# Attention and a feed-forward layer in one kernel: weights' sign by a leaky ReLU in whole words, chunks made when due, TensorE transposes for the second group

## The chip, the core and the metric

The kernel runs on one core of a Trainium2 chip. A core has five engines that run side by side and wait for each other through semaphores: PE (TensorE, matmul), DVE (VectorE), ACT (ScalarE), POOL (GpSimd) and SP (SyncE, which here issues every DMA). The metric is device time of one execution in microseconds (us).

## The reference

```python
def _attn_ref(q, k, v):                      # B, H, S, D = 8, 8, 576, 64
    scores = matmul(q, k.T) / sqrt(D)
    rel = pos[:, None] - pos[None, :]
    mask_local = (rel >= 0) & (rel < 32)                 # heads 0 to 3
    mask_strided = (rel >= 0) & (same position mod 32)   # heads 4 to 7
    attn = softmax(where(mask, scores, -1e9))
    return matmul(attn, v)

def reference(q, k, v, w_in, w_out):
    x = attn_out as (4608, 512)
    h = x @ w_in                             # (512, 2048)
    g = h * sigmoid(1.702 * h)
    return g @ w_out                         # (2048, 512)
```

The two weight matrices come as float64 (q, k and v as float32).

## The kernel before

**Feed-forward.** The 4608 tokens are cut into 12 groups of 384, the 2048 hidden units into 16 blocks of 128. One *step* is one block for one group: `ffn1` is 12 matmuls of 384 columns into a bank `h`, `act` makes `g` from it (tanh on ACT, a product on DVE) and splits it into a high part `gh` (ACT) and a low part `gl` (POOL in the first 8 steps, else DVE), and two steps later `ffn2` is 9 matmuls of 512 columns into three banks `o`. There are 192 steps, first 8 blocks of group 0, then the 16 of group 1, then the other 8 of group 0, then group after group.

**Attention.** It is done in 48 *pairs* of blocks of queries, and each group needs four pairs on average. A pair goes through: `scores` (PE, into `s`; mask and row maximum on DVE), `softmax` (eight Exp on ACT with a row sum each; `rinv` on DVE; a product on POOL), `transpose` of `pr` into `pt`, and `values` (PE, into `a`; ACT and DVE split it into the high and low inputs `xh`, `xl` of `ffn1`; a last letter `l` or `s` tells local from strided). Two buffers `pr` take turns. Pairs 0 to 4 (group 0) are done ahead of the steps and use TensorE transposes (`t`, L206) followed by a DVE copy (L210); the later ones use DVE's own 32x32 block transposes (L220). Pairs 5 to 9, which group 1 needs, are transposed at steps 1 to 5; pairs 10 and 11 are transposed from step 25 on.

**Weights.** They come in 32 *chunks* (w_in and w_out alternating, 16 each; 128 rows of 512 doubles). A chunk is loaded as pairs of 32-bit words (`raw`); the high word holds sign, exponent and the top of the mantissa, the low word the rest. `bits_w` makes the low word hold the sign bit at the top and three mantissa bits at the bottom: L299 writes its lower half and L302 its upper half, both on ACT as 16-bit elements at a step of 8 bytes. `join_w` scales the high word as a float into `t` (L312, DVE), which rebases the exponent, and shifts and ORs the two (L316, DVE). `split_w` splits the float32 into a high part (L329, ACT cast to fp32r) and a low part (L330, DVE). A generator does this piece by piece: `fill(n)` advances it by n pieces, three to a chunk.

**Order.** Instructions are recorded in program order and a scheduler with a simulated timeline then orders each engine's queue; from the first step on (`in_order`), PE's matmuls are kept in program order. Each engine executes its queue in order.

Of the kernel before, what the change touches and what calls it, by code (L numbers as in the profile page):

```python
# [9 lines left out]
F32 = mybir.dt.float32  # L10
F32R = mybir.dt.float32r
U32 = mybir.dt.uint32
U8 = mybir.dt.uint8
BF16 = mybir.dt.bfloat16
F16 = mybir.dt.float16
U16 = mybir.dt.uint16
AF = mybir.ActivationFunctionType
ALU = mybir.AluOpType
AX = mybir.AxisListType
# [21 lines left out]
HU = HEADS * U  # L41

AHEAD = 2
LAG = 2
RAWB = 3
NEARLY = 4
PF = (2, 3, 3, 3, 3, 3, 4)
F0F = 6
NH = NF // 2


# [23 lines left out]
def attn_ffn(ctx, tc, qk, vs, w_in, w_out, masks, ident, out):  # L75
    nc = tc.nc
# [20 lines left out]
    pairs, windows, n0 = _pairs()  # L97
    in_order = [False]

    def matmul(*args, **kw):  # L100

        ins = nc.tensor.matmul(*args, **kw)  # L102
        if in_order[0]:
            tc.keep_in_program_order(ins)

# [2 lines left out]
    def load_qk(p):  # L108
        if p < len(pairs) and p not in qks:
            qks[p] = st4([P, 2, 2, U, P], F32, f"qk_{p}")  # L110
            nc.sync.dma_start(out=qks[p], in_=qk[p])
# [10 lines left out]

    prs = [const.tile([P, HU, P], F32, name=f"pr_{i}") for i in range(AHEAD)]
    pts = {
# [15 lines left out]
    def scores(p):  # L140

        nq, nk, mask = geom(p)
        t = qks[p]
        sps = [bank(f"s{j}_{p}") for j in range(2)]
        for g in range(2):
            for u in range(U):
                for j in range(2):
                    rows = slice(j * D, (j + 1) * D)
                    i = g * U + u
                    matmul(  # L150
                        sps[j][:nq, i * nk : (i + 1) * nk],
                        lhsT=t[rows, 0, g, u, :nq],
                        rhs=t[rows, 1, g, u, :nk],
                        start=True,
                        stop=True,
                    )
        scale = 1.0 / np.sqrt(D)
        pr = prs[p % AHEAD]
        n = mask.shape[1]
        for j in range(2):  # L160
            o = pr[:nq, j * 2 * U : (j + 1) * 2 * U, :nk]
            if n == 2:
                o = o.rearrange("p (g u) n -> p g (u n)", g=2)
            nc.vector.scalar_tensor_tensor(
                out=o, in0=sps[j][:nq, : 2 * U * nk].rearrange("p (a n) -> p a n", a=n),
                scalar=scale, in1=mask, op0=ALU.mult, op1=ALU.add,
            )
        nmax = small.tile([P, HU], F32, tag="nmax", name=f"nmax_{p}")
        nc.vector.tensor_reduce(  # L169
            out=nmax[:nq], in_=pr[:nq, :, :nk], axis=AX.X, op=ALU.max, negate=True  # L170
        )
        nmaxs[p] = nmax

    def softmax(p):

        nq, nk, _ = geom(p)
        nmax, pr = nmaxs.pop(p), prs[p % AHEAD]
        ssum = small.tile([P, HU], F32, tag="ssum", name=f"ssum_{p}")
        for i in range(HU):
            nc.scalar.activation(  # L180
                pr[:nq, i, :nk], pr[:nq, i, :nk], AF.Exp,
                bias=nmax[:nq, i : i + 1], scale=1.0,
                accum_out=ssum[:nq, i : i + 1],
            )
            if i % 2 and i < HU - 1:
                yield
        rinv = small.tile([P, HU], F32, tag="rinv", name=f"rinv_{p}")
        nc.vector.tensor_scalar_add(out=rinv[:nq], in0=ssum[:nq], scalar1=1e-9)  # L188
        nc.vector.reciprocal(out=rinv[:nq], in_=rinv[:nq])  # L189
        nc.gpsimd.tensor_tensor(  # L190
            out=pr[:nq, :, :nk],
            in0=pr[:nq, :, :nk],
            in1=rinv[:nq].unsqueeze(2).broadcast_to([nq, HU, nk]),
            op=ALU.mult,
        )

    def transpose(p):
        nq, nk, _ = geom(p)
        kind, pr = pairs[p][0], prs[p % AHEAD]
        pt = pts[kind]  # L200
        if p < n0:
            for j in range(2):
                tps = bank(f"t{j}_{p}")
                heads = slice(j * 2 * U, (j + 1) * 2 * U)
                for i in range(2 * U):
                    nc.tensor.transpose(  # L206
                        tps[:nk, i * nq : (i + 1) * nq], pr[:nq, j * 2 * U + i, :nk],
                        ident_sb[:nq, :nq],
                    )
                nc.vector.tensor_copy(  # L210
                    out=pt[:nk, heads, :nq],
                    in_=tps[:nk, : 2 * U * nq].rearrange("p (h n) -> p h n", h=2 * U),
                )
            return


        for qb in range(-(-nq // BL)):
            for kb in (qb, qb + 1) if kind == "l" else range(max(qb - 1, 0), qb + 1):
                i, o = slice(qb * BL, (qb + 1) * BL), slice(kb * BL, (kb + 1) * BL)
                nc.vector.transpose(out=pt[o, :, i], in_=pr[i, :, o])  # L220
# [53 lines left out]
    raws = {}  # L274

    order = [(f, m) for f in range(NF) for m in range(2)]
# [12 lines left out]

    words = {}  # L290

    def bits_w(i):

        raw = raws[i]
        l16 = raw.bitcast(U16)
        nc.scalar.activation(  # L299
            l16[:, :, 0], raw.bitcast(U8)[:, :, 3], AF.Copy, scale=1 / 32, bias=-15.5 / 32  # L300
        )
        nc.scalar.activation(  # L302
            raw.bitcast(F16)[:, :, 1], raw.bitcast(F32)[:, :, 1], AF.Copy, scale=2.0**-80
        )

    def join_w(i):
        raw = raws.pop(i)
        h, l = raw[:, :, 1], raw[:, :, 0]
        t = words[i] = st2([P, DM], U32, f"t_{i}")


        nc.vector.tensor_scalar_mul(  # L312
            out=t.bitcast(F32), in0=h.bitcast(F32), scalar1=2.0**-112
        )
        yield
        nc.vector.scalar_tensor_tensor(  # L316
            out=t, in0=t, scalar=3, in1=l, op0=ALU.logical_shift_left, op1=ALU.bitwise_or
        )
# [11 lines left out]
        nc.vector.tensor_tensor(out=lo, in0=v, in1=hi.bitcast(F32), op=ALU.subtract)  # L330

    def weights():
        for i in range(RAWB):
            load_w(i)
        bits_w(0)
        for i in range(len(order)):
            if i + 1 < len(order):
                bits_w(i + 1)
            yield from join_w(i)
            yield  # L340
            load_w(i + RAWB)
            split_w(i)
            yield

    wgen = weights()

    def fill(n):
        for _ in range(n):
            next(wgen, None)

    hps = {}

# [14 lines left out]
    def act(j, f):  # L367
# [6 lines left out]
        gh, gl = (  # L374
            ffn.tile([P, G], F32R, tag=f"g{x}", name=f"g{x}_{j}_{f}", bufs=LAG + 1) for x in "hl"
        )
# [51 lines left out]
    def run(gen, n=HU):  # L428
        for _ in range(n):
            next(gen, None)  # L430
# [3 lines left out]
    load_qk(1)  # L434
    ident_sb = const.tile([P, P], F32, name="ident_sb")
    nc.sync.dma_start(out=ident_sb, in_=ident)
    next(wgen)
    for i in range(n0 + 2):
        if i < n0:
            load_qk(i + 1)  # L440
            load_v(i)
            scores(i)
            run(softmax(i))
        if 0 <= i - 2:
            values(i - 2)
        if 0 <= i - 1 < n0:
            transpose(i - 1)
        fill(PF[i])
        if i >= n0 - 2:
            ffn1(0, i - n0 + 2, (0, 1))  # L450
    load_v(n0)
    for p in range(n0, n0 + AHEAD):
        load_qk(p)
        scores(p)
        run(softmax(p))
    load_qk(n0 + AHEAD)

# [6 lines left out]
    due = {}  # L464
    p = n0
# [8 lines left out]

    in_order[0] = True
    late, turn = None, {p: s for s, p in due.items()}
    for s in range(len(steps) + LAG):
        cur = steps[s] if s < len(steps) else None
        old = steps[s - LAG] if s >= LAG else None
        p, q = due.get(s), due.get(s - 1)  # L480
        if cur:
            ffn1(*cur, tuple(range(2 if s < NEARLY else 0, NC)))
            act(*cur)
        if late is not None:
            run(late[0], -(-4 // (late[1] - s)) if late[1] > s else HU)
        if p is not None:
            load_v(p)
            load_qk(p + AHEAD)
            transpose(p)
        if q is not None:  # L490
            values(q)
            load_v(q + 1)
            if q + AHEAD < len(pairs):
                scores(q + AHEAD)
                load_qk(q + AHEAD + 1)
                if late is not None:
                    run(late[0])
                late = softmax(q + AHEAD), turn[q + AHEAD]
                run(late[0], 1)
        fill(F0F)  # L500
        if old:
            for parts in ((0, 1, 2),) if old[1] == NF - 1 else ((0, 1), (2,)):
                for i in range(NT):
                    ffn2(*old, i, parts)
            gs.pop(old)


def _layout(q, k, v, w_in, w_out):
# [73 lines left out]
```

## Time and profile before

| | |
|---|---|
| median of 3 runs | 996.97 us (996.59 to 997.46) |
| the profiled execution | 997.53 us, of which the span is 995.7 us |
| PE busy | 946.0 us, 95% of the span |
| DVE, ACT, POOL busy | 560.2, 453.3, 96.9 us |
| HBM traffic | 54.69 MB read, 9.44 MB written |

The page of the profile shows busy time in 40 slices of 24.9 us each, one digit a slice, in tenths. A group row names line, engine, operation, tiles, shape and count, then the busy time in us and the mean of one instruction in ns, then the idle time of the engine before them and who ended it. The timeline has start, duration, engine, line, tile and count; the chain of waits lists what set the end, in order of time. A table by stages has, for each stretch, its length and each engine's busy time, then the granted TensorE clock (1.00 is full), the DMA engines' busy share and GB/s.

### The profile page before, as it was taken

The numbers are of one execution on the slowest core, as the hardware profiler recorded it, in microseconds if no ns is written. First come the engines' busy times: TensorE is split into PE (matmuls) and PEld (weight loads), VectorE is DVE, ScalarE is ACT, GpSimd is POOL, SyncE is SP. The second block draws the span as 40 slices with busy tenths as digits, with TensorE's granted clock in tenths as the row PEclk, the third lists the DMA queues.
The fourth block names the chain that finished last, engine by engine and source line by source line (L and its number), as shares of the span: only waits on it lengthen the run. The fifth ranks groups of instructions, "written<-read, shape, count | busy, mean of one in ns | idle before, by whom it ended". The sixth has DMA issues, their size and how long they took to land.

```text
span 995.7 us, 14642 instructions
## 1 busy us (share of the span) xinstructions
PE 946.0 (95%) x5608; PEld 834.5 (84%) x5608; DVE 560.2 (56%) x1071; ACT 453.3 (46%) x1334; POOL 96.9 (10%) x64
## 2 busy tenths in 40 slices
PE   4787779999999999999999999999999999999998
PEld 4665568988888888889888888889888888889997
DVE  5789984246665755634555665644555666422322
ACT  6999993224444344332344444332344444322221
POOL 2112220001011011100010110100010110000000
PEclk9997799999999999999999999999999999999999
DMA  8455520011311212210212212110212120000000
GB/s 301 159 191 179 195 83 1 1 62 35 96 41 56 87 41 65 65 32 1 96 32 65 75 54 64 65 32 1 81 47 65 65 64 22 33 1 1 32 1 32
DMA packets 23973, 65.06 MB, mean 65 GB/s; under 512 B 2656, under 2 KB 2912, under 8 KB 23904
## 3 DMA queue, kind: packets, MB, share of 16 engines
q1 hardware_dynamic: 23904, 64.14, 19.5%
q8 instruction: 44, 0.72, 0.3%
q14 instruction: 25, 0.20, 0.1%
HBM read 54.69 MB, written 9.44 MB: 64 GB/s over the span
## 4 chain that ended last, share of the span: by engine, by line
PE 85%; ACT 10%; DVE 3%; issue 1%; DMA 1%; SPq 0%
PE o L102 40%; PE h L102 38%; PE s L102 3%; ACT pr L180 3%; PE a L102 3%; ACT raw L299 3%; ACT raw L302 3%; DVE t L316 1%; DMA raw<-w_in 1%; DVE t L312 1%; ACT o L329 1%; ACT i L329 0%; DVE pt_s L220 0%; DVE pt_l L220 0%; ACT g L370 0%
## 5 line engine op out<-in xcount | busy, mean ns | idle before, releaser
L102 PE MATMUL o<-o,gh 128*128 128x512 f32 x1152 | 312.1, 403 | 8.1 <-ACT gh L377 7.6
L102 PEld LDWEIGHTS o<-o,gh 128*128 128x128 f32 x1152 | 212.9, 190 | 50.0 <-ACT gh L377 8.7
L102 PE MATMUL h<-xhl,i 128*128 128x384 f32 x768 | 234.8, 347 | 1.8 <-DVE g L371 1.4
L102 PE MATMUL h<-xhs,i 128*128 128x384 f32 x768 | 226.8, 336 | 2.2 <-ACT xhs L268 2.2
L371 DVE SCALAR_TENSOR_TENSOR g<-g,h 128x384 f32<-128x384 f32 x192 | 106.4, 554 | 207.4 <-ACT g L370 206.4
L370 ACT ACTIVATE g<-h 128x384 f32<-128x384 f32 x192 | 93.9, 489 | 273.4 <-PE h L102 205.4
L180 ACT ACTIVATE pr<-pr,nmax 96x128 f32<-96x128 f32 (+2 forms) x384 | 143.5, 378 | 102.2 <-DVE nmax L169 102.2
L102 PE MATMUL o<-o,gl 128*128 128x512 f32 x576 | 172.0, 401 | 1.4 <-POOL gl L379 1.4
L379 DVE TENSOR_TENSOR gl<-g,gh 128x384 fp32r<-128x384 f32 x184 | 120.1, 653 | 74.6 <-ACT gh L377 74.1
L377 ACT CAST gh<-g 128x384 fp32r<-128x384 f32 x192 | 98.8, 515 | 129.2 <-DVE g L371 129.1
L190 POOL TENSOR_TENSOR pr<-pr,rinv 96x1024 f32<-96x1024 f32 (+2 forms) x48 | 84.6, 1762 | 724.8 <-DVE rinv L189 699.0
L102 PEld LDWEIGHTS h<-xhl,i 128*128 128x128 f32 x768 | 144.5, 192 | 11.4 <-DVE g L371 1.9
L102 PEld LDWEIGHTS h<-xhs,i 128*128 128x128 f32 x768 | 142.2, 189 | 2.5 <-ACT xhs L268 2.4
L102 PEld LDWEIGHTS o<-o,gl 128*128 128x128 f32 x576 | 109.8, 191 | 28.3 <-POOL gl L379 1.8
L102 PE MATMUL h<-xll,i 128*128 128x384 f32 x384 | 131.5, 342 | 0.0
L102 PE MATMUL h<-xls,i 128*128 128x384 f32 x384 | 128.9, 336 | 0.1
L102 PEld LDWEIGHTS h<-xll,i 128*128 128x128 f32 x384 | 73.6, 192 | 8.5
L102 PE MATMUL s<-qk 64*96 64x128 f32 (+2 forms) x768 | 65.6, 295 | 11.0 <-DMA qk<-qk 8.7
L102 PEld LDWEIGHTS h<-xls,i 128*128 128x128 f32 x384 | 72.4, 189 | 0.5 <-DVE xls L270 0.4
L180 ACT ACTIVATION_READ_ACCUMULATOR pr<-pr,nmax 96x1 f32 (+2 forms) x384 | 72.7, 189 | 0.0
L102 PEld LDWEIGHTS s<-qk 64*96 64x96 f32 (+2 forms) x768 | 54.0, 184 | 19.2 <-issue 7.3
L188 DVE TENSOR_SCALAR rinv<-ssum 96x8 f32<-96x8 f32 (+2 forms) x48 | 8.0, 167 | 99.5 <-ACT pr L180 99.5
(39 smaller groups left out, 604.3 us busy)
## 6 DMA issues: line engine op xcount, KB each, us to landing
qk<-qk SPq DMA_DIRECT2D x48, 512.0 KB, 4.2
v<-vs SPq DMA_DIRECT2D x48, 256.0 KB, 2.6
out<-out SPq DMA_DIRECT2D x36, 256.0 KB, 2.1
raw<-w_in SPq DMA_DIRECT2D x16, 512.0 KB, 4.8
raw<-w_out SPq DMA_DIRECT2D x16, 512.0 KB, 5.5
masks_sb<-masks SPq DMA_DIRECT2D x1, 96.0 KB, 3.4
ident_sb<-ident SPq DMA_DIRECT2D x1, 64.0 KB, 5.3
```

The costliest lines, as they stand in the source:

```text
L102: ins = nc.tensor.matmul(*args, **kw)
L180: nc.scalar.activation(pr[:nq, i, :nk], pr[:nq, i, :nk], AF.Exp, bias=nmax[:nq, i : i + 1], scale=1.0, accum_out=ssum[:nq, i : i + 1],)
L190: nc.gpsimd.tensor_tensor(out=pr[:nq, :, :nk], in0=pr[:nq, :, :nk], in1=rinv[:nq].unsqueeze(2).broadcast_to([nq, HU, nk]), op=ALU.mult,)
L299: nc.scalar.activation(l16[:, :, 0], raw.bitcast(U8)[:, :, 3], AF.Copy, scale=1 / 32, bias=-15.5 / 32)
L302: nc.scalar.activation(raw.bitcast(F16)[:, :, 1], raw.bitcast(F32)[:, :, 1], AF.Copy, scale=2.0**-80)
L312: nc.vector.tensor_scalar_mul(out=t.bitcast(F32), in0=h.bitcast(F32), scalar1=2.0**-112)
L316: nc.vector.scalar_tensor_tensor(out=t, in0=t, scalar=3, in1=l, op0=ALU.logical_shift_left, op1=ALU.bitwise_or)
L329: nc.scalar.copy(out=hi, in_=v)
L370: nc.scalar.activation(g2, ps[:, :G], AF.Tanh, scale=0.851)
L371: nc.vector.scalar_tensor_tensor(out=g2, in0=g2, scalar=1.0, in1=ps[:, :G], op0=ALU.add, op1=ALU.mult)
L377: nc.scalar.copy(out=gh, in_=g2)
L379: eng.tensor_tensor(out=gl, in0=g2, in1=gh.bitcast(F32), op=ALU.subtract)
```

## The change

Five things are edited.

- `bits_w` and `join_w` become `words_w`. ACT scales the high word with a leaky ReLU (Prelu, L304 of the new kernel) into `t`: positive inputs by 2^-112, negative ones by 2^-112 times 2^32, so that a negative number's exponent carries an extra bit that the later shift moves to the sign's place. ACT's second operation (L307) writes the three mantissa bits as a whole 32-bit word. DVE's scaling (L312) is gone; DVE's shift-and-OR (now L310) stays.
- `split_to(n)` makes whole chunks up to number n: 7 before the first step, then three for every two steps up to 16, then one a step. Before it was two a step until all were made. Four raw chunks are loaded ahead, not three.
- Pairs 5 to 9 are transposed by TensorE and copied by DVE (`NPE = 10`), the matmuls at the end of the step, behind `ffn2`.
- Those transposes are kept in PE's program order from the first step on (`transposed`).
- `scores` of a pair is recorded at most 11 steps ahead of its transpose (`SOON`): for pairs 10 and 11 that is step 14 and 17, before it was 5 and 6; pairs 24 and 36 move by four steps; the others stay.

```diff
-RAWB = 3
+RAWB = 4
-PF = (2, 3, 3, 3, 3, 3, 4)
-F0F = 6
+NPE = 10
+EARLY = (0, 1, 2, 3, 4, 5, 7)
...
-        if p < n0:
+        if p < NPE:
...
-    def bits_w(i):
-        raw = raws[i]
-        l16 = raw.bitcast(U16)
-        nc.scalar.activation(
-            l16[:, :, 0], raw.bitcast(U8)[:, :, 3], AF.Copy, scale=1 / 32, bias=-15.5 / 32
-        )
-        nc.scalar.activation(
-            raw.bitcast(F16)[:, :, 1], raw.bitcast(F32)[:, :, 1], AF.Copy, scale=2.0**-80
-        )
-
-    def join_w(i):
+    def words_w(i):
         raw = raws.pop(i)
         h, l = raw[:, :, 1], raw[:, :, 0]
         t = words[i] = st2([P, DM], U32, f"t_{i}")
-        nc.vector.tensor_scalar_mul(
-            out=t.bitcast(F32), in0=h.bitcast(F32), scalar1=2.0**-112
-        )
-        yield
+        nc.scalar.activation(
+            t.bitcast(F32), h.bitcast(F32), AF.Prelu, scale=2.0**-112, alpha=2.0**32
+        )
+        nc.scalar.activation(
+            l, raw.bitcast(U8)[:, :, 3], AF.Copy, scale=1 / 32, bias=-15.5 / 32
+        )
         nc.vector.scalar_tensor_tensor(
             out=t, in0=t, scalar=3, in1=l, op0=ALU.logical_shift_left, op1=ALU.bitwise_or
         )
...
-        fill(F0F)
+        split_to(max(min(EARLY[-1] + (s + 1) * 3 // 2, 2 * NH), 2 * NH + s - 5))
         if old:
             for parts in ((0, 1, 2),) if old[1] == NF - 1 else ((0, 1), (2,)):
                 for i in range(NT):
                     ffn2(*old, i, parts)
             gs.pop(old)
+        if p is not None and p < NPE:
+            transpose(p)
```

Three places in the engines' queues show what moves. The first is ACT ahead of the steps, where the attention of group 0 is still being made. Before:

```order
L299 ACTIVATE raw_320<-raw_320 128x512
L299 ACTIVATE raw_397<-raw_397 128x512
L329 CAST i_399<-t_394 128x512
L302 ACTIVATE raw_320<-raw_320 128x512
L302 ACTIVATE raw_397<-raw_397 128x512
L329 CAST o_441<-t_436 128x512
L268 CAST xhl_235<-a_292 128x2x192
L180 ACTIVATE pr_84,ssum_279<-pr_84,nmax_277 90x90 x8
```

and now, at the same pair:

```order
L323 CAST i_430<-t_383 128x512
L323 CAST o_459<-t_424 128x512
L184 ACTIVATE pr_84,ssum_271<-pr_84,nmax_269 90x90 x8
L272 CAST xhl_228<-a_284 128x2x192
L304 ACTIVATE t_453<-raw_311 128x512
L304 ACTIVATE t_462<-raw_387 128x512
L307 ACTIVATE raw_457<-raw_457 128x512
L307 ACTIVATE raw_466<-raw_466 128x512
```

A chunk is still three ACT instructions (two to make the words, one cast), and they still stand between one pair's softmax and the next one's. The second place is PE from step 3 to step 4. Before:

```order
L102 MATMUL o_0_693<-o_322,gh_1_587 128x512 x2
L102 MATMUL o_1_696<-o_322,gh_1_587 128x512 x2
L102 MATMUL o_2_699<-o_322,gh_1_587 128x512 x2
L102 MATMUL o_0_693<-o_322,gl_1_588 128x512
L102 MATMUL o_1_696<-o_322,gl_1_588 128x512
L102 MATMUL o_2_699<-o_322,gl_1_588 128x512
L102 MATMUL h_4_796<-xhl_235,i_571 128x384
```

and now:

```order
L101 MATMUL o_0_679<-o_389,gh_1_596 128x512 x2
L101 MATMUL o_1_682<-o_389,gh_1_596 128x512 x2
L101 MATMUL o_2_685<-o_389,gh_1_596 128x512 x2
L101 MATMUL o_0_679<-o_389,gl_1_597 128x512
L101 MATMUL o_1_682<-o_389,gl_1_597 128x512
L101 MATMUL o_2_685<-o_389,gl_1_597 128x512
L106 MATMUL t_7_778<-ident_sb,pr_84 90x90 x4
L106 MATMUL t_7_784<-ident_sb,pr_84 90x90 x4
L101 MATMUL h_4_790<-xhl_228,i_566 128x384
```

Eight transposes of pair 7 stand between the `o` matmuls and the next step's `h`. The third place is DVE in the same steps, before:

```order
L316 SCALAR_TENSOR_TENSOR t_874<-t_874,raw_768 128x512
L312 TENSOR_SCALAR t_884<-raw_778 128x512
L270 TENSOR_TENSOR xll_747<-a_737,xhl_746 128x2x192
L220 STREAM_TRANSPOSE pt_s<-pr_84 32x8x32 x5
L316 SCALAR_TENSOR_TENSOR t_884<-t_884,raw_778 128x512
L330 TENSOR_TENSOR i_879<-t_874,i_879 128x512
```

and now:

```order
L310 SCALAR_TENSOR_TENSOR t_1032<-t_1032,raw_858 128x512
L173 TENSOR_REDUCE nmax_755<-pr_83 96x8
L367 SCALAR_TENSOR_TENSOR g_0_3_709<-g_0_3_709,h_3_471 128x384
L214 COPY pt_s<-t_7_778 90x4x90
L214 COPY pt_s<-t_7_784 90x4x90
L310 SCALAR_TENSOR_TENSOR t_1070<-t_1070,raw_933 128x512
L324 TENSOR_TENSOR i_1076<-t_1032,i_1076 128x512
```

Two copies stand where five block transposes stood, and no L312 is left. The new program has one load of the activation table, as the old one has.

More of the change, by code (lines that the diff above doesn't have):

```diff
@@ L14 @@
 BF16 = mybir.dt.bfloat16
-F16 = mybir.dt.float16
-U16 = mybir.dt.uint16
 AF = mybir.ActivationFunctionType
@@ L43 @@
 AHEAD = 2
+SOON = 11
 LAG = 2
-RAWB = 3
+RAWB = 4
 NEARLY = 4
-PF = (2, 3, 3, 3, 3, 3, 4)
-F0F = 6
+NPE = 10
+EARLY = (0, 1, 2, 3, 4, 5, 7)
 NH = NF // 2
@@ L102, in matmul, with transposed @@
         ins = nc.tensor.matmul(*args, **kw)
+        if in_order[0]:
+            tc.keep_in_program_order(ins)
+    def transposed(*args):
+        ins = nc.tensor.transpose(*args)
         if in_order[0]:
@@ L205, in transpose @@
                 for i in range(2 * U):
-                    nc.tensor.transpose(
+                    transposed(
                         tps[:nk, i * nq : (i + 1) * nq], pr[:nq, j * 2 * U + i, :nk],
@@ L334, in weights, with split_to @@
             load_w(i)
-        bits_w(0)
+        yield 0
+        words_w(0)
         for i in range(len(order)):
             if i + 1 < len(order):
-                bits_w(i + 1)
-            yield from join_w(i)
-            yield
+                words_w(i + 1)
             load_w(i + RAWB)
             split_w(i)
-            yield
+            yield i + 1
     wgen = weights()
-    def fill(n):
-        for _ in range(n):
-            next(wgen, None)
+    made = [-1]
+    def split_to(n):
+        while made[0] < min(n, len(order)):
+            made[0] = next(wgen)
     hps = {}
@@ L436, in attn_ffn @@
     nc.sync.dma_start(out=ident_sb, in_=ident)
-    next(wgen)
+    split_to(0)
     for i in range(n0 + 2):
@@ L447, in attn_ffn @@
             transpose(i - 1)
-        fill(PF[i])
+        split_to(EARLY[i])
         if i >= n0 - 2:
@@ L476, in attn_ffn @@
     late, turn = None, {p: s for s, p in due.items()}
+    begins = {}
+    for p in range(n0 + AHEAD, len(pairs)):
+        begins[max(turn[p - AHEAD] + 1, turn[p] - SOON)] = p
     for s in range(len(steps) + LAG):
@@ L479, in attn_ffn @@
         old = steps[s - LAG] if s >= LAG else None
-        p, q = due.get(s), due.get(s - 1)
+        p, q, r = due.get(s), due.get(s - 1), begins.get(s)
         if cur:
@@ L488, in attn_ffn @@
             load_qk(p + AHEAD)
-            transpose(p)
+            if p >= NPE:
+                transpose(p)
         if q is not None:
@@ L492, in attn_ffn @@
             load_v(q + 1)
[L493 to L499, printed above, removed]
-        fill(F0F)
+        if r is not None:
+            scores(r)
+            load_qk(r + 1)
+            if late is not None:
+                run(late[0])
+            late = softmax(r), turn[r]
+            run(late[0], 1)
+        split_to(max(min(EARLY[-1] + (s + 1) * 3 // 2, 2 * NH), 2 * NH + s - 5))
         if old:
@@ L505, in attn_ffn @@
             gs.pop(old)
+        if p is not None and p < NPE:
+            transpose(p)
 def _layout(q, k, v, w_in, w_out):
```

## The prediction

> **What bounds the kernel now.** I read the slices of the page first, then the table by stages, then the chain of waits in the stage where PE is not full, and last the order of the instructions on ACT.
>
> ```profile
> PE   4787779999999999999999999999999999999998
> ACT  6999993224444344332344444332344444322221
> ```
>
> ```profile
> 0.00:9.20 9.20, 3.46 (x25) 3.14 (x27) 1.29 (x2) 1.28 (x1) 3.61 (x8) 1.00 0.79 273
> 9.20:66.00 56.80, 41.20 (x235) 34.19 (x231) 44.53 (x82) 56.76 (x142) 8.67 (x5) 1.00 0.59 212
> 66.00:149.80 83.80, 59.16 (x341) 48.37 (x341) 76.10 (x139) 82.20 (x182) 22.29 (x15) 0.82 0.45 155
> 149.80:992.00 842.20, 842.19 (x5012) 748.77 (x5012) 437.55 (x848) 313.01 (x1011) 62.35 (x36) 1.00 0.14 44
> ```
>
> The columns are length, then PE, PEld, DVE, ACT and POOL busy, clock, DMA share, GB/s. From 149.8 to 992.0 PE is busy for all of 842.2 us: there the edits can gain nothing, and lose only what PE is given to do. From 9.2 to 149.8 ACT is busy for 139.0 of 140.6 us, PE for 100.4. All that can be won lies there. Its marks in the timeline:
>
> ```profile
> 9.21 1.35 ACT L299 ACTIVATE raw<-raw 128x512 uint16<-128x512 uint8 x1 [7.20 <-DMA raw<-w_in]
> 66.48 0.44 PE L102 MATMUL h<-xhs,i 128*128 128x384 f32 x1 [2.22 <-ACT xhs L268]
> 146.19 0.48 ACT L370 ACTIVATE g<-h 128x384 f32<-128x384 f32 x1
> 149.78 2.15 PE L102 MATMUL o<-o,gh 128*128 128x512 f32 x6 [2.17 <-ACT gh L377]
> ```
>
> ACT starts on the first raw chunk at 9.2; PE gets group 0's whole input at 66.5; the `g` of step 8 (first of group 1) starts at 146.2; PE starts the `o` of that block at 149.8 and is never idle again. Call this last moment T. Behind it both kernels have the same work but for two `scores`, so the new time is the old one, less the 149.8 - T, plus those.
>
> What ACT's work costs per instruction stands in the chain of waits, where instructions of one queue overlap less than their durations say:
>
> ```profile
> 31.17 0.37 ACT xhl L268
> 31.54 2.96 ACT pr L180 x16
> 34.50 2.39 ACT raw L299 x2
> 37.23 2.46 ACT raw L302 x2
> 45.70 0.42 ACT i L329
> 46.12 0.51 ACT o L329
> 96.33 0.32 ACT gh L377
> 97.92 0.49 ACT g L370
> 155.81 2.10 PE o L102 x9
> 157.91 2.11 PE h L102 x12
> ```
>
> A softmax takes 2.96 us of ACT, a half-word operation 1.21, a cast 0.47, an `xh` 0.37, `gh` and `g` 0.32 and 0.49. **A test of these prices**: ahead of the `g` of step 8, ACT's order holds 63 half-word operations, 29 weight casts, 12 softmaxes, 16 `xh` and 8 `g` with 8 `gh`: 76.2 + 13.6 + 35.5 + 5.9 + 6.5 = 137.7, and 9.2 + 137.7 = 146.9, where the trace has 146.2. Ahead of group 0's last `xh` stand 28, 11, 6 and 6: 59.1, so 68.3 for the 66 measured. The sum of ACT's queue explains the whole stretch.
>
> **The change part by part.**
>
> *Words.* The operations concerned, grouped up to 150 us:
>
> ```profile
> L299 ACT ACTIVATE raw<-raw 128x512 uint16<-128x512 uint8 x32 | 43.4, 1390 | 7.2 <-DMA raw<-w_in 7.2
> L302 ACT ACTIVATE raw<-raw 128x512 f16<-128x512 f32 x32 | 42.5, 1368 | 0.1
> L329 ACT CAST i<-t 128x512 fp32r<-128x512 f32 x16 | 10.3, 642 | 0.5 <-DVE t L316 0.5
> L312 DVE TENSOR_SCALAR t<-raw 128x512 f32<-128x512 f32 x31 | 18.0, 587 | 1.6 <-DMA raw<-w_in 1.5
> ```
>
> L299 reads bytes and L302 words, yet they take the same 1390 and 1368 ns: reading does not make them slow. Both write 16-bit elements at a step of 8 bytes. L329, as many elements, writes adjacent whole words in 642. L312 reads the same high words at the same step in 587, on DVE. Prelu (L304) reads like L302 and writes like L329, so I price it as L329: 0.47 on the queue, 1.21 at worst. L307 writes whole words, but still at a step of 8 bytes; no row shows such a write. Bounds 0.47 and 1.21; I take 0.47, since the only slow ones are part-word writes, and keep 1.21 as a rival.
>
> The Trainium skill (ScalarE: Activation LUTs, What ACT_TABLE_LOAD costs) gives 186 ns + 0.833 ns an element for any function, fp32 and bf16 alike, 613 ns here; L329 agrees with it, L299 and L302 take more than twice that, so the page does not hold for them and cannot say which of width and step is to blame. Its Rules for kernel authors put a multiplication on VectorE, not ScalarE, against this edit; that matters where the words win nothing, a rival below.
>
> *Sums for the new order.* Ahead of group 0's last `xh` ACT now has 12 Prelu and 15 copies, 11 casts, 6 softmaxes, 6 `xh`: 12.7 + 5.2 + 17.8 + 2.2 = 37.9, so PE gets its input at 47.1, not 66. Ahead of the `g` of step 8: 29 and 32, 28 casts, 10 softmaxes, 16 `xh`, 16 `g` and `gh`: 28.7 + 13.2 + 29.6 + 5.9 + 6.5 = 83.9, so 93.1, not 146.9. Of these 53.8 us, 47.5 come from the words, 5.9 from the two softmaxes moved behind, and next to nothing from "chunks made when due": the scheduler still has 28 of 32 casts there (before 29).
>
> *What comes next.* With ACT at 93.1 PE is close. Its rows:
>
> ```profile
> 27.48 1.54 PE L206 MATMUL t<-ident_sb,pr 96*128 96x96 f32 x8 [0.49 <-POOL pr L190]
> 86.80 0.88 PE L102 MATMUL a<-pt_l,v 128*64 128x96 f32 x16 [0.75 <-DVE g L371]
> 87.61 1.12 PE L102 MATMUL s<-qk 64*96 64x128 f32 x16
> ```
>
> From group 0's input to T PE has 108 `h` at 2.11/12 (19.0), 72 `o` at 2.10/9 (16.8), five `values` (4.4), three `scores` (3.4), and the new five transposes at 1.54 (7.7): 51.3, so T is at least 98. From the `h` of step 8 to its `o` lie two steps of 4.2, so ACT's sum gives at least 93.1 + 8.4 = 101.5. The old kernel could not see this, as PE was ahead.
>
> The transposes now stand in PE's order, and behind them wait the next `h`, `values` and all that follows. What they wait for:
>
> ```profile
> L164 DVE SCALAR_TENSOR_TENSOR pr<-s,masks_sb 90x360 f32<-90x360 f32 x32 | 16.0, 519 | 0.0
> L169 DVE TENSOR_REDUCE nmax<-pr 90x8 f32<-90x720 f32 x16 | 14.3, 891 | 0.2
> L190 POOL TENSOR_TENSOR pr<-pr,rinv 90x720 f32<-90x720 f32 x16 | 23.1, 1441 | 232.6 <-DVE rinv L189 232.6
> L379 POOL TENSOR_TENSOR gl<-g,gh 128x384 fp32r<-128x384 f32 x8 | 8.8, 1103 | 27.6 <-ACT gh L377 27.6
> ```
>
> For pair 7 two L164, L169, a softmax, the product and a `gl` ahead of it on POOL are 1.04 + 0.89 + 2.96 + 1.44 + 1.10 = 7.4 us without any queueing; PE has between its `scores` and its transposes 2.1 + 1.5 + 1.05 + 0.9 + 1.1 + 2.1 = 8.8 us to do. Each place behind a chunk's piece on ACT or DVE is thus nearly all PE waiting, at steps 3 to 5.
>
> DVE's relief and load up to 150 us:
>
> ```profile
> L220 DVE STREAM_TRANSPOSE pt_l<-pr 32x256 f32<-32x256 f32 x18 | 7.8, 434 | 0.2
> L220 DVE STREAM_TRANSPOSE pt_s<-pr 32x256 f32<-32x256 f32 x17 | 7.4, 433 | 0.2
> L210 DVE COPY pt_l<-t 128x384 f32<-128x384 f32 x4 | 2.2, 546 | 0.0
> ```
>
> Of its 120.6 us (44.5 + 76.1) go 18.0 (L312) and 15.2 (L220), and ten copies of 0.55 come: 92.9, less the two moved pairs. That is as much as ACT has. So three engines near their limits pass work to and fro, and none will run without waits. Loads are nearer too: a DMA share of 0.59 over 56.8 us becomes 0.88 in the 38 us left, below the 1.02 here:
>
> ```profile
> 10.00:15.00 5.00, 0.72 (x4) 0.37 (x2) 2.87 (x5) 4.97 (x11) 0.00 (x0) 1.00 1.02 412
> ```
>
> The waits on top of 101.5 lie between none and the 24.6 us that PE was idle from 66 to 149.8 (83.8 - 59.2). I take half, 12.5: T = 114.
>
> *Moved behind T*: `scores` of pairs 10 and 11, 2 x 1.1 = 2.2 us of PE, where PE is never idle; their masks and softmaxes are covered by DVE and ACT (437.6 and 313.0 of 842.2 us). The four-step moves of pairs 24 and 36 cost nothing for the same reason.
>
> **The sum**: the profiled execution took 997.5 (995.7 of span, 1.8 around it), 0.5 above the median. 997.5 - (149.8 - 114) + 2.2 = 963.9: 964 us.
>
> **Rivals.**
>
> *L307 stays slow* (the step, not the width, is the price). 32 x 0.74 more on ACT: 116.8 for the `g` of step 8, ACT alone the bound as before, 3.6 from there to T as now, and some 5 of waits: T = 125, 975 us. For it: no whole-word write at that step in any row. Against it: as above.
>
> *The words win nothing*, the change does not do what it says: both at 1.21, 138.2 + 3.6: T = 142, 992 us. Against it speaks L329.
>
> *DVE, POOL and the pairs' chain become the bound*: all 24.6 us of waits, T = 126, 976 us. For it DVE's 92.9.
>
> *Slower: PE at half rate.* The first matmuls behind T start 0.32 us apart, later ones 0.18:
>
> ```profile
> 153.01 0.52 PE L102 MATMUL h<-xhl,i 128*128 128x384 f32 x1
> 153.33 0.52 PE L102 MATMUL h<-xll,i 128*128 128x384 f32 x1
> 158.81 0.33 PE L102 MATMUL h<-xhs,i 128*128 128x384 f32 x1
> 158.99 0.33 PE L102 MATMUL h<-xls,i 128*128 128x384 f32 x1
> ```
>
> and the stage from 66 to 149.8, with PE idle in between, had a clock of 0.82. If the five transposes interrupt PE so often that it stays slow, the 43.6 us without them become 1.8 x 43.6 = 78.4; with 24.6 of idle time T = 47.1 + 24.6 + 7.7 + 78.4 = 157.8, 1008 us. It decides from T = 147.6 on, when 71% of the stretch are at half rate. Against it: PE's 51 us of work fill three quarters of the 67 us from 47 to 114. The Trainium skill (TensorE: Matmul & The Clock Gate, What's actually happening) has the array half-clocked until it has been busy for a window of about 3.4 us; the 0.32 and 0.18 agree.
>
> **How the numbers follow.** Chances: as forecast 0.66 (952 to 973: waits from none to 22), L307 slow 0.14, chain or DVE bound 0.10, words win nothing 0.06, slower 0.04. The time is the likeliest's, 964; the range reaches over the second and third to 981, and down to 952 where nothing waits. A measurement of this kernel can tell 0.2%, about 2 us, from no change. Faster holds all cases but the last and a bit of the fourth: 0.94; no change 0.02; slower 0.04.
>
> **What would show it.** In the new profile: L304 and L307 near 650 ns (L307 near 1390 is the first rival); group 0's input on PE near 47 to 50; the `g` of step 8 at 95 to 105; PE without idle time from about 114; ACT's slices below 9 ahead of that; PE waiting for POOL's `pr` at the transposes of pairs 7 to 9; from T on PE full and some 844 us long. I am wrong if T lies outside 101 to 128, or if PE is idle behind it.

## The result and the profile after

The changed kernel takes 970.77 us in the median (968.12 to 970.96, 4 runs) against 996.93 (996.59 to 997.46) of the kernel before beside it: a ratio of 0.9731, with a 95% interval of 0.9714 to 0.9748. It is faster by 26.2 us; the forecast was 964 us, between 952 and 981. The profiled execution took 970.86 us, with a span of 969.1.

The slices of its page, 24.2 us each:

```profile
PE   4997999999999999999999999999999999999998
ACT  6878933243434443333343443332443444222221
PEclk9998999999999999999999999999999999999999
```

ACT is at 9 in one slice (96.9 to 121.1), where it was in five; PE is at 9 from the second slice on, but for one dip and the last slice. The table by stages (columns as in the prediction), cut at the moments that the prediction speaks of, shows the same in numbers:

```profile
9.20:59.80 50.60, 41.16 (x234) 34.59 (x232) 38.26 (x69) 42.92 (x149) 11.47 (x6) 1.00 0.66 236
59.80:121.90 62.10, 53.98 (x350) 45.72 (x350) 53.53 (x92) 55.16 (x146) 17.75 (x13) 0.95 0.53 192
9.20:121.90 112.70, 95.14 (x583) 80.30 (x581) 91.80 (x160) 98.08 (x294) 29.22 (x18) 0.97 0.59 212
121.90:966.00 844.10, 843.45 (x5045) 748.68 (x5043) 444.53 (x858) 317.48 (x1039) 65.68 (x38) 1.00 0.14 45
```

The marks in the timeline:

```profile
9.06 0.67 ACT L304 ACTIVATE t<-raw 128x512 f32<-128x512 f32 x1 [7.05 <-DMA raw<-w_in]
57.84 0.52 ACT L272 CAST xhs<-a 128x240 fp32r<-128x240 f32 x2
59.81 0.52 PE L101 MATMUL h<-xhs,i 128*128 128x384 f32 x1
101.86 0.44 PE L101 MATMUL h<-xhl,i 128*128 128x384 f32 x1 [0.19 <-DVE xll L274]
114.89 0.48 ACT L366 ACTIVATE g<-h 128x384 f32<-128x384 f32 x1
121.88 1.56 PE L101 MATMUL o<-o,gh 128*128 128x512 f32 x6
```

Group 0's whole input reaches PE at 59.8 (call it x; before 66.5), T is 121.9 (before 149.8), and PE is never idle from 101.9 on. From T to the end PE is full for 844 us. The groups of ACT up to 150 us, and the chain of waits:

```profile
L307 ACT ACTIVATE raw<-raw 128x512 uint32<-128x512 uint8 x32 | 21.2, 672 | 0.5 <-DMA raw<-w_out 0.5
L304 ACT ACTIVATE t<-raw 128x512 f32<-128x512 f32 x32 | 21.1, 672 | 8.5 <-DMA raw<-w_in 7.0 <-DVE o L324 1.0 <-DVE i L324 0.4
```

```profile
15.15 0.57 ACT raw L307
19.88 0.56 ACT t L304
138.87 1.05 PE s L101 x16
152.74 1.05 PE s L101 x16
```

Both whole-word operations take 672 ns where the half-word ones took 1390 and 1368, and 0.56 on the queue where those took 1.21. The two moved `scores` stand behind T with 1.05 us each, 2.1 in all.

**Where the time came from.** The sum's own form, 997.5 - (149.8 - T) + 2.2, gives 971.8 with the T measured; the profiled execution took 970.9. So the gain is the 27.9 us by which T is earlier, less the two `scores`, as forecast. But T is 7.9 us later than the 114 of the forecast, and x is 12.7 later than its 47.1.

### The profile page after: what moved, and what is told of

It is laid out like the page before. It is cut to its first block, busy times and chain, and to the rows that moved or that the text cites. A ratio compares the mean times of both kernels' runs of the same rounds, so it can differ in the third digit from the quotient of the medians.

```text
span 969.1 us, 14677 instructions
## 1 busy us (share of the span) xinstructions
PE 942.1 (97%) x5648; PEld 832.2 (86%) x5648; DVE 538.9 (56%) x1020; ACT 417.0 (43%) x1334; POOL 98.5 (10%) x64
## 4 chain that ended last, share of the span: by engine, by line
PE 93%; DVE 3%; ACT 2%; DMA 1%; issue 1%; SPq 0%; POOL 0%; DVEq 0%; POOLq 0%
PE h L101 42%; PE o L101 42%; PE s L101 5%; PE a L101 4%; ACT pr L184 1%; DVE t L310 1%; DMA raw<-w_out 1%; PE t L106 1%; DVE pr L168 1%; DVE nmax L173 0%; DVE i L324 0%; POOL pr L194 0%; ACT raw L307 0%; ACT o L323 0%; DVE pt_l L214 0%
## 5 line engine op out<-in xcount | busy, mean ns | idle before, releaser
L101 PE MATMUL o<-o,gh 128*128 128x512 f32 x1152 | 308.4, 400 | 0.7 <-DVE xls L274 0.7
L101 PEld LDWEIGHTS o<-o,gh 128*128 128x128 f32 x1152 | 210.6, 188 | 41.4 <-issue 1.1
L101 PE MATMUL o<-o,gl 128*128 128x512 f32 x576 | 169.4, 395 | 0.0
L375 DVE TENSOR_TENSOR gl<-g,gh 128x384 fp32r<-128x384 f32 x184 | 122.7, 667 | 74.8 <-ACT gh L373 74.2
L101 PE MATMUL s<-qk 64*96 64x128 f32 (+2 forms) x768 | 61.7, 287 | 11.3 <-DMA qk<-qk 11.3
L101 PEld LDWEIGHTS s<-qk 64*96 64x96 f32 (+2 forms) x768 | 50.9, 177 | 19.6 <-DVE i L324 5.9
```

Source lines behind the costliest of these rows:

```text
L375: eng.tensor_tensor(out=gl, in0=g2, in1=gh.bitcast(F32), op=ALU.subtract)
```

## What makes x late

Two views show it. First, PE's work up to x is the same as before: 41.16 us of busy time here from 9.2 to x, and 41.20 in the stage from 9.2 to 66.0 of the kernel before. It was hidden behind ACT there; here the two are nearly even (ACT is busy for 42.9 us of that stretch). 9.2 + 41.2 is already 50.4, and PE was idle for another 9.4. The waits of PE in that stretch (the times are sum, count, longest):

```profile
PE s L101 <- DMA qk<-qk: 5.6, 1, 5.6
PE a L101 <- DVE pt_l L214: 2.2, 1, 2.2
PE t L106 <- POOL pr L194: 1.7, 1, 1.7
```

All three end by 33.9. From there PE runs without a wait to x, and all of it at half rate (the first row stands ahead of it, for comparison):

```profile
16.26 1.78 PE L101 MATMUL s<-qk 64*108 64x108 f32 x16 [5.60 <-DMA qk<-qk]
33.90 1.69 PE L106 MATMUL t<-ident_sb,pr 108*108 108x108 f32 x8 [1.67 <-POOL pr L194]
36.42 1.77 PE L101 MATMUL s<-qk 64*108 64x108 f32 x8
48.81 2.02 PE L101 MATMUL s<-qk 64*96 64x128 f32 x8
56.32 1.47 PE L101 MATMUL a<-pt_s,v 90*64 90x90 f32 x16
66.42 0.42 PE L101 MATMUL h<-xhs,i 128*128 128x384 f32 x1
66.68 0.34 PE L101 MATMUL h<-xls,i 128*128 128x384 f32 x1
```

Eight matmuls of a `scores` take 2.02 us at 48.8 and a `values` 1.47 at 56.3; the same ones take 1.11 and 0.84 where a run below has them at full rate (three loaded ahead, 48.70 and 49.74). A single `h` takes 0.52 at x (59.81); the first of 0.34 comes at 66.7. The clock column of the table does not show this: it has 1.00 there. The trace's own clock records begin only at 66.39 us, with the change to full, and the column counts full where there is no record yet. Where there are records they agree with the spacing of the matmuls (half from 83.46 to 90.28).

The rate is not all of it. Eight matmuls of a `scores` that stand apart in PE's order take as long as sixteen in a row: at half rate and 64x108, 1.77 us at 36.42 for eight and 1.78 at 16.26 for sixteen. The `scores` of pairs 5 and 6 stand in such pieces ahead of x (eight, six and two, then eight and eight) and take 7.6 us of PE's queue from start to start; sixteen in a row of each would take 3.7 (an estimate: 1.71 from the row at 16.26 to the next, and 1.95 for sixteen of 64x96 at half rate in the run with the words alone, at 94.91). No run changes this alone.

The last `values` of group 0, on which x rests, start at 56.3 in PE's order and are done at 57.8. ACT, which has a softmax and four instructions of chunks to do from 52.7 on, is free for the last `xhs` at 57.84, so that the two queues meet there. PE then has partial `h` to do until x, and by then ACT's `xhs` has been done since 58.36.

Second, ACT now waits for the others. Its waits from 9.2 to 60, the first of which ends at 9.06 and counts for nothing here:

```profile
ACT t L304 <- DMA raw<-w_in: 7.0, 1, 7.0
ACT xhs L272 <- PE a L101: 3.1, 1, 3.1
ACT o L323 <- DVE t L310: 2.4, 3, 1.2
ACT i L323 <- DVE t L310: 1.5, 1, 1.5
ACT t L304 <- DVE i L324: 0.4, 1, 0.4
```

7.4 us of waits for PE and DVE, and 27 whole-word operations at 0.56 to 0.57 and not 0.47 (2.6 us), make 10.0 of the 11.3 by which ACT's last `xh` of group 0 ends late (58.4, forecast 47.1).

DVE's part at x itself is one stretched operation, first its group up to 150 us, then the timeline:

```profile
L324 DVE TENSOR_TENSOR i<-t,i 128x512 fp32r<-128x512 f32 x16 | 12.7, 791 | 0.5 <-ACT i L323 0.4
```

```profile
58.65 1.88 POOL L194 TENSOR_TENSOR pr<-pr,rinv 108x864 f32<-108x864 f32 x1 [12.91 <-DVE rinv L193]
58.95 2.11 DVE L324 TENSOR_TENSOR i<-t,i 128x512 fp32r<-128x512 f32 x1
60.99 0.58 DVE L274 TENSOR_TENSOR xls<-a,xhs 128x240 fp32r<-128x240 f32 x2
```

L324 takes 0.79 us in the mean; this one ran beside a product of POOL, and behind it `xls` came late, for which PE waited 1.11. The next L310, at 62.80 beside POOL's next product, takes 2.39 us, where the one at 58.40 took 0.64. The Trainium skill (GPSIMD Engine Reference, Specifications) says that GpSimd's way to SBUF is shared with VectorE and that instructions with two SBUF inputs contend for it; these rows fit, and no run here tests it apart.

## The experiments

Each stands beside runs of the kernel before on its own chip. PE's time up to T, from the table by stages of each run (busy and idle us; T; the sum's form with that T; the profiled execution):

| run | 9.2 to x: busy, idle | x | x to T: busy, idle | T | sum | measured |
|---|---|---|---|---|---|---|
| the change | 41.2, 9.4 | 59.8 | 54.0, 8.1 | 121.9 | 971.8 | 970.9 |
| all but the words | 36.5, 27.3 | 73.0 | 57.0, 15.9 | 145.9 | 995.8 | 996.0 |
| the words alone | 37.5, 6.6 | 53.3 | 56.2, 16.3 | 125.8 | 973.5 | 972.4 |
| block transposes | 41.2, 9.4 | 59.8 | 52.8, 13.0 | 125.6 | 975.5 | 974.6 |
| two chunks a step | 35.7, 11.0 | 55.9 | 54.0, 9.5 | 119.4 | 969.3 | 968.4 |
| three loaded ahead | 36.9, 6.9 | 53.0 | 54.6, 8.8 | 116.4 | 966.3 | 965.4 |
| warmed PE | 36.1, 13.9 | 59.1 | 52.3, 6.8 | 118.2 | 968.1 | 967.2 |
| no partial `ffn1` | 35.4, 10.3 | 54.9 | 57.7, 8.6 | 121.2 | 971.1 | 970.2 |
| scores behind | 34.2, 13.3 | 56.7 | 52.8, 13.0 | 122.5 | 972.4 | 971.5 |
| three ahead, two a step | 41.5, 5.8 | 56.5 | 54.6, 7.8 | 118.9 | 968.8 | 967.9 |
| three ahead, warmed | 35.1, 14.0 | 58.3 | 52.5, 6.6 | 117.4 | 967.3 | 966.4 |

(For the words alone the 2.2 is left out, since the `scores` are not moved.) In every run the sum's form is within 1.1 us of the time: nothing behind T matters but the two `scores`.

**All but the words.** The new kernel with the old half-word operations and DVE's scaling (calls in short form, here and in the next run):

```diff
-        nc.scalar.activation(t, h, AF.Prelu, scale=2.0**-112, alpha=2.0**32)
-        nc.scalar.activation(l, raw.bitcast(U8)[:, :, 3], AF.Copy, ...)
+        nc.scalar.activation(raw.bitcast(U16)[:, :, 0], raw.bitcast(U8)[:, :, 3], AF.Copy, ...)
+        nc.scalar.activation(raw.bitcast(F16)[:, :, 1], raw.bitcast(F32)[:, :, 1], AF.Copy, scale=2.0**-80)
+        nc.vector.tensor_scalar_mul(out=t, in0=h, scalar1=2.0**-112)
```

> The new kernel with the old way of making words: two half-word operations on ACT and DVE's scaling; chunks when due, TensorE transposes and late scores stay. Theory (the words carry the gain): ACT's queue ahead of the g of step 8 grows by 61 x 0.74 = 45 us and bounds the start again, T near 142, 990 to 994 us. Rival (the other edits carry half of the 26 us): 984 us or less.

Measured: 995.89 us against 997.09, 0.9995 (0.9986 to 1.0004), no change. The row of its first stage shows ACT full, as before:

```profile
9.20:50.00 40.80, 23.03 (x160) 19.36 (x157) 30.15 (x52) 40.77 (x96) 7.05 (x4) 1.00 0.62 230
```

ACT is busy for 40.77 of 40.80 us, and T is 145.9, later than the 142 of the theory, so that the time lies just above its 990 to 994. The other edits move it by 3.9 us at the old prices, of which the moved `scores` take 2.2 back.

**The words alone.** The old kernel with the new operations in the place of the old:

```diff
-        nc.scalar.activation(l16[:, :, 0], raw.bitcast(U8)[:, :, 3], AF.Copy, ...)
-        nc.scalar.activation(raw.bitcast(F16)[:, :, 1], raw.bitcast(F32)[:, :, 1], AF.Copy, scale=2.0**-80)
...
-        nc.vector.tensor_scalar_mul(out=t, in0=h, scalar1=2.0**-112)
+        nc.scalar.activation(t, h, AF.Prelu, scale=2.0**-112, alpha=2.0**32)
+        nc.scalar.activation(l, raw.bitcast(U8)[:, :, 3], AF.Copy, ...)
```

> The old kernel with the new words alone (Prelu and a whole-word copy on ACT, no scaling on DVE). Theory: ACT's queue ahead of the g of step 8 is 63 x 0.47 + 13.6 + 35.5 + 5.9 + 6.5 = 91, at 100 us; two steps of 4.2 and waits as in the new kernel (20): T near 129, 974 to 979 us. Rival (the edits need each other, DVE's block transposes and the dense pace eat the relief): 985 us or more.

Measured: 973.15 us, 0.9761 (0.9747 to 0.9775), a gain of 23.9 us. With the run above this closes the square: nothing 997, the rest alone 996, the words alone 973, both 971. The words carry the gain. Without them the rest wins nothing that can be measured; with them it seems to add some 3 us, but the two intervals just touch (from 0.9747 on, and up to 0.9748), so that this is likely and not shown.

**Block transposes.** Pairs 5 to 9 by DVE's transposes again:

```diff
-NPE = 10
+NPE = 5
```

> The new kernel with DVE's block transposes for pairs 5 to 9. Theory (from 60 us on PE's own queue is the bound): PE is spared 40 transposes, some 5 us, and waits some 2 more for DVE: 966 to 969 us. Rival (DVE and the pairs' chain are the bound): DVE gets 9.7 us more, 974 to 978 us.

Measured: 974.60 us, 0.9767 (0.9753 to 0.9780), which lies outside the interval of the change: TensorE's transposes are worth 0.0036, about 3.6 us. The rival came, not the theory. x is the same, but from there to T PE does 1.2 us less and waits 4.9 more. Its waits in that stretch:

```profile
PE a L101 <- issue: 7.1, 2, 4.8
PE o L101 <- DVE xls L274: 3.8, 1, 3.8
```

and those of the change itself, all that reach half a microsecond:

```profile
PE h L101 <- DVE g L367: 3.5, 1, 3.5
PE t L106 <- DVE pt_l L214: 1.1, 1, 1.1
PE h L101 <- DVE xls L274: 1.1, 1, 1.1
PE o L101 <- DVE xls L274: 0.7, 1, 0.7
PE a L101 <- DVE pt_l L214: 0.6, 1, 0.6
```

Without TensorE's transposes two `values`, whose `pt` DVE makes there, wait for 7.1 us (the view names no releaser), and an `o` for DVE's `xls`. PE's additional work is more than paid by less waiting.

**Two chunks a step**, the old pace, so that chunks are not "made when due":

```diff
-        split_to(max(min(EARLY[-1] + (s + 1) * 3 // 2, 2 * NH), 2 * NH + s - 5))
+        split_to(EARLY[-1] + 2 * (s + 1))
```

> The new kernel with two chunks a step until all are made, as before. Theory (the scheduler places chunks by its own timeline, the recorded pace matters little): 969 to 973 us, as the new kernel. Rival (a slower pace frees ACT and DVE in the first steps): 976 us or more.

Measured: 968.69 us, 0.9723 (0.9709 to 0.9736); the interval overlaps that of the change. The pace is worth nothing that can be measured, as the prediction had it.

**Three loaded ahead** undoes the fourth raw chunk:

```diff
-RAWB = 4
+RAWB = 3
```

> The new kernel with three raw chunks loaded ahead, not four. Theory (loads are not on the path): 969 to 972 us. Rival (pair 2's queries and keys, for which PE waits 5.6 us until 16.3, come earlier behind fewer chunks): 967 us or less.

Measured: 965.48 us against 996.44, 0.9691 (0.9678 to 0.9704), which is faster than the change, and the best of all runs. The 969 to 972 of the theory did not come, the time of the rival did. The start of pair 2's softmax on ACT, and PE's matmuls up to x:

```profile
23.48 0.38 ACT L184 ACTIVATE pr<-pr,nmax 108x108 f32<-108x108 f32 x1
```

```profile
15.03 1.78 PE L101 MATMUL s<-qk 64*108 64x108 f32 x16 [4.26 <-DVE rinv L192]
44.72 0.98 PE L106 MATMUL t<-ident_sb,pr 90*90 90x90 f32 x8
48.70 1.11 PE L101 MATMUL s<-qk 64*96 64x128 f32 x8
49.74 0.84 PE L101 MATMUL a<-pt_s,v 90*64 90x90 f32 x16
53.00 0.45 PE L101 MATMUL h<-xhs,i 128*128 128x384 f32 x1 [1.18 <-ACT xhs L272]
```

In the change `scores` of pair 2 start at 16.26 behind a load, here at 15.03 behind DVE, so the rival's earlier load gives 1.2 us at most there. In the change ACT has 11 instructions of chunks between the softmaxes of pairs 1 and 2 (from 19.77) and starts on the second at 26.79; here it has 6 and starts at 23.48. That this is because fewer raw chunks are there to work on is argued, not shown. PE's own run to x then starts 2.7 us earlier (31.17, not 33.90), and at 45.1 by the clock records PE changes to full rate, 21 us earlier than in the change: busy time up to x falls by 4.3, idle time by 2.5, x by 6.8.

**Warmed PE.** 29 matmuls that nobody reads (bf16, on the masks) are added: 18 behind `scores` of pair 1, then 6 and 5, to see how much the half rate costs. PE's matmuls are also kept in program order up to the 18, so the order of the others behind them changes too.

```diff
+            in_order[0] = i < 2
...
+            if i == 1:
+                busy(18)
+                in_order[0] = False
+            if i == 3:
+                busy(5)
...
+            if i == 1:
+                busy(6)
```

> The new kernel with 29 more matmuls of 384 columns whose result nobody reads, in PE's empty time at the start: 18 behind the scores of pair 1, 6 behind the transposes of pair 0, 5 behind the scores of pair 3. In the new kernel PE's matmuls stand 0.32 us apart until 66 us and 0.18 after, and PE is never idle from 36 to 60. Theory (PE at half rate sets group 0's input at 60 us): if the added work brings PE to its full rate and it stays there, the matmuls between 34 and 58 shrink by up to 10 us, group 0's input comes at 50 to 55, and the time is 961 to 967 us. Rival (the pairs' chain through ACT, DVE and POOL sets it): 969 to 973 us, or slower by the 5 us that the added work takes.

Measured: 967.67 us, 0.9711 (0.9698 to 0.9724); the interval just overlaps that of the change, and the time lies between the two that were expected. The timeline of PE:

```profile
9.71 4.10 PE L101 MATMUL warm<-masks_sb 128*128 128x384 bf16 x18
15.84 1.01 PE L101 MATMUL s<-qk 64*108 64x108 f32 x16 [2.03 <-DMA qk<-qk]
31.74 1.69 PE L106 MATMUL t<-ident_sb,pr 108*108 108x108 f32 x8
59.08 0.69 PE L101 MATMUL h<-xhs,i 128*128 128x384 f32 x1 [6.53 <-ACT xhs L272]
```

The 18 matmuls raise the rate (sixteen `s` at 15.84 in 1.01, where the change takes 1.78), but later it is lost again (eight `t` at 31.74 in 1.69, as in the change). By the clock records it is full from 11.8 to 25.4 and from 42.5 to 56.2. PE's last `values` of group 0 are then done by 52.6, yet x comes at 59.1: PE waits 6.5 us for ACT, whose order puts two softmaxes and nine instructions of chunks ahead of that `xhs`. So x is only 0.7 us earlier with the rate raised for part of the time: ACT's order is the next limit, right behind PE.

**No partial `ffn1`.** The `h` of group 0 that can be made from the local heads alone are moved behind x:

```diff
-NEARLY = 4
+NEARLY = 0
...
-        if i >= n0 - 2:
-            ffn1(0, i - n0 + 2, (0, 1))
```

> The new kernel without the 24 first-half matmuls of steps 0 to 3 ahead of group 0's full input; they run at their steps. Theory (PE's queue sets the input's time): 18 of them, 6 us at half rate, no longer stand ahead of the last values, the input comes at 53 to 55 us, and the 24 cost 4.2 us later at full rate: 967 to 971 us. Rival (PE was idle time there that the partial work filled for nothing): 974 us or more.

Measured: 970.43 us, 0.9736 (0.9722 to 0.9749): no difference from the change, though x comes 4.9 us earlier. The rows from x to T:

```profile
54.90:121.20 66.30, 57.74 (x367) 49.89 (x368) 55.85 (x93) 57.13 (x153) 17.88 (x13) 0.95 0.51 175
```

Instead of 350 matmuls in 54.0 us PE has 367 in 57.7. Of the 5.8 us that PE is busy for less ahead of x, 3.7 come back behind it, and 1.4 of more idle time; T is 0.7 earlier, which does not show in the time.

**Scores behind.** `scores` of pairs 5 and 6 stand behind the last `values` of group 0 in PE's order:

```diff
+        in_order[0] = i > n0
```

> The new kernel with the scores of pairs 5 and 6 (group 1) kept behind the last values of group 0 on PE. Theory (they take 7.5 us of PE at half rate ahead of the values): group 0's input at 53 to 55 us, not 60; group 1's pairs start later, so the time moves by less, 966 to 972 us. Rival (the input's time does not follow PE's queue): input still at 60 us, 972 us or more.

Measured: 970.68 us, 0.9738 (0.9725 to 0.9751): the same again, with x 3.1 us earlier. Here the gift is lost to a wait; PE's waits from x to T, and the timeline:

```profile
PE t L106 <- POOL pr L194: 6.9, 2, 5.4
```

```profile
62.51 1.88 POOL L194 TENSOR_TENSOR pr<-pr,rinv 108x864 f32<-108x864 f32 x1 [16.22 <-DVE rinv L193]
64.43 1.69 PE L106 MATMUL t<-ident_sb,pr 108*108 108x108 f32 x8 [5.39 <-POOL pr L194]
```

Pair 5's product on POOL starts at 62.51, not at 58.65, and its transposes, which stand in PE's order, wait 5.4 us for it. PE is idle for 13.0 us, not 8.1.

**Two combinations of the best one.** Three loaded ahead with two chunks a step:

> Three raw chunks loaded ahead and two chunks a step: the two settings of the old kernel in the new one, with the new words, TensorE transposes and late scores. Theory (both settings help or do nothing, each acts at its own place: the load depth before group 0's input, the pace after it): 963 to 966 us. Rival (they were the same gain twice, a matter of where the scheduler happens to put things): 967 to 971 us.

Measured: 966.63 us against 996.99, 0.9701 (0.9683 to 0.9719), between the two that were expected and not better than three ahead alone. And three ahead with the 29 unread matmuls:

> Three raw chunks loaded ahead, with the 29 unread matmuls in PE's empty time at the start. With three ahead alone PE is at half rate until 44.7 us and group 0's input comes at 53.0. Theory (what is left of PE's half rate before 44.7 still costs): input at 49 to 52 us, 961 to 964 us. Rival (from there on the pairs' chain through ACT, DVE and POOL sets it): input at 52 us or later, 965 us or more.

Measured: 967.46 us, 0.9720 (0.9700 to 0.9739). The rival came: the gains don't add. PE is idle for 14.0 us ahead of x and busy for 35.1, of which 7.8 are the unread work.

## The prediction, point by point

**What bounds the kernel** was right: ACT, ahead of T. The run with all but the words leaves ACT full ahead of x (63.7 of 63.8 us) and wins nothing.

**The price of a whole word** was right: 672 ns, near the forecast 650, and 0.56 on the queue where 0.47 was put, well below 1.21. The rival that L307 stays slow falls: at the same step of 8 bytes a whole word costs half of what a half-word does. The rival that the words win nothing falls with it. The small difference counts 61 times: 61 x 0.09 = 5.5 us more for ACT ahead of the `g` of step 8.

**Moved behind T** was right: 2.1 us for 2.2, and PE full for 844 us. The pace of the chunks counted for nothing, as said.

**"PE gets its input at 47.1" is the step that failed.** It took the sum of ACT's queue alone, and PE's work was added up only from there on. The row of the old stage from 9.2 to 66 had PE busy for 41.20 us beside ACT's 56.76; with ACT's sum at 37.9, PE was the longer of the two, and 9.2 + 41.2 = 50.4 was the least at PE's old rate and order. With PE's 9.4 us of waits, 59.8 was measured. The test of ACT's prices on the old kernel was sound, but it held only while ACT was last.

**The waits** were put wrong in place and size. From x to T the prediction had 114 - 47.1 = 66.9 us; it took 62.1. Of that PE is busy 54.0, 2.7 more than the 51.3 of the sum, and idle 8.1. The error of 12.7 ahead of x and one of 4.8 the other way behind it leave T 7.9 late. On the 101.5 of the prediction the waits are 20.4 and not 12.5, within the 22 that bounded the forecast, and T lies within 101 to 128.

That the forecast of T was not further off is in part luck. Its base of 101.5 is ACT's sum and two steps. PE's own sum over the old rows is 9.2 + 41.2 + 51.3 = 101.7, the same by chance, so that leaving PE out ahead of x did not move the base. What was too small by it are the waits: they were taken from PE's idle time behind x, and the 9.4 us of idle time ahead of x were put at nothing. 101.7, 17.5 us of idle time in all and the 2.7 of more work give the 121.9. T also does not follow x: without partial `ffn1` x is 4.9 us earlier and T 0.7, and with scores behind x is 3.1 earlier and T 0.6 later.

**DVE and the chain of pairs.** The forecast 92.9 us of DVE's work compare with 91.8 from 9.2 to T. PE, DVE and ACT are busy for 95.1, 91.8 and 98.1 of 112.7 us, so that no one is the bound and each waits for the others, as the prediction said of three engines near their limits. The rival by which all of the 24.6 us are waits (T = 126) didn't come; only in the two runs with DVE's block transposes and the new words is T as late as that (125.6 and 125.8).

**PE at half rate** was a rival for the stretch behind x. There some 13 of 62 us are at half rate (59.8 to 66.4 and, by the clock records, 83.5 to 90.3), far from the 71% from which it decided. Ahead of x, where nothing was charged for it, it is all of the time.

**The signs.** ACT's slices below 9 came but for one, PE without idle time behind 114 too (from 101.9 on). The `g` of step 8 came at 114.9, not at 95 to 105, yet ahead of its `o`: PE was in its own work by then. PE did not wait for POOL's `pr` at pairs 7 to 9; behind x its longest wait is 3.5 for DVE's `g`.

**What stays open.** Why PE reaches full rate at 45.1 in one kernel and at 66.4 in another, and so a part of the gain of three loaded ahead, was not settled. That PE's rate by itself changes the time was not shown either: the interval of warmed PE overlaps that of the change, and its matmuls are ordered otherwise. What the split `scores` cost ahead of x was not tested. Moving x alone gained nothing in two runs; what the fourth chunk costs by its place in ACT's order and what by PE's rate was not told apart.

## What to carry to other kernels

When an edit relieves the engine that bounds a stage, set every other engine's busy time in that same stage against the new sum, before adding anything: here the row with PE's 41.20 us had been quoted, and it alone moved the input from 47.1 to 50.4 at that rate and order. Idle time belongs into the sum for each stage, the one in which the old bound hid it included. On ACT, writes of parts of words cost twice what whole words at the same step do, so bit work is worth recasting into 32-bit results. And more buffers are not always faster: here three raw chunks ahead beat four by some 4 to 5 us, perhaps because with four ACT's work on later chunks stands in front of what the chain of pairs needs.

## What was not expected of the hardware

- Half-word writes at a step of 8 bytes take 1390 and 1368 ns for 512 elements, whole-word writes at that step 672, and adjacent words 620 to 642. The step costs next to nothing, the width half.
- Prelu with an alpha of 2^32 costs no more than a copy: 672 ns for both.
- Long unbroken work does not by itself bring PE to full rate: from 33.9 to 66.4 us it stays at half, with one gap of 1.1 us. In the run with three loaded ahead the same matmuls change at 45.1, and with 18 dense bf16 matmuls the change comes 2.1 us after the first of them (11.8, from 9.7). The Trainium skill (TensorE: Matmul & The Clock Gate, What's actually happening) has the full clock after a busy window of about 3.4 us; the 18 matmuls agree, the 32 us of attention and `ffn1` do not.
- The clock records of a trace begin with the first change, and the granted clock of the table reads 1.00 before it; ahead of that the spacing of matmuls is the better reading. Between two changes lies a multiple of 3.41 us in every trace of this case (17.07 and 6.83 here, 13.66 and 17.06 in warmed PE).
